# Scores beside the value product, loads reordered, another opening and a one-pass last eviction: windowed attention followed by a SoLU layer

## The chip, the cores and the metric

The kernel runs on one core of a Trainium2 chip. The metric is the device time of one execution in microseconds; several runs give a median. The engines of the core are TensorE (PE, with its weight loads shown as PEld), VectorE (DVE), ScalarE (ACT), GpSimd (POOL) and SyncE (SP, which issues the DMAs). Each works through its own list of instructions in order, and they wait for each other by semaphores.

## The reference

Eight heads of eight sequences of 576 positions attend within a window of 32 (heads 0 to 3), or to every fourth position of a window of 128 (heads 4 to 7). The result, 4608 tokens of 512 values, goes through a layer whose hidden activation is h times softmax(h), followed by a layer norm.

```python
scores = scale * np.matmul(q, k.transpose(0, 1, 3, 2))
...
scores = np.where(masks[None, :, :, :], scores, -1000000000.0)
scores = scores - np.max(scores, axis=-1, keepdims=True)
attn = np.exp(scores)
attn = attn / (np.sum(attn, axis=-1, keepdims=True) + 1e-09)
return np.matmul(attn, v).astype(np.float32)
...
h = x @ w_in                                  # 4608 x 512 x 1024
h_max = np.max(h, axis=-1, keepdims=True)
e = np.exp(h - h_max)
sm = e / (np.sum(e, axis=-1, keepdims=True) + 1e-09)
solu = h * sm
mu = np.mean(solu, axis=-1, keepdims=True)
var = np.mean((solu - mu) ** 2, axis=-1, keepdims=True)
ln = (solu - mu) / np.sqrt(var + 1e-06) * g_ln
return (ln @ w_out).astype(np.float32)        # 4608 x 1024 x 512
```

The weights come as float64.

## The kernel before

**Tiling.** The attention is cut into 32 units: a unit n is two heads of one sequence, and n % 4 of 2 and 3 are the dilated heads. The tokens are cut into 36 tiles i of 128 for the layer. Unit n's result fills a stretch of a ring (`x_hi`, `x_lo`) of two sequences; tile i reads 128 tokens of it over all four units of a sequence. Matrix products of the layer are done in three terms (high by high, high by low, low by high part), so a tile has 24 matmuls of 512 columns for `w_in` and 24 for `w_out`.

**Words.** The program is written out as a list of words, and each word issues the instructions of one small function (the table `one`, line 494). For a unit n: `q` and `v` load it on SP; `S` (line 175) are its scores, 80 small matmuls of 64 rows by 32 columns, into PSUM banks 2 and 3; `mask`, `max`, `sum`, `inv`, `norm`, `turn` are VectorE's; `sub` is POOL's from unit 4 on; `exp` ScalarE's; `V` (line 253), 96 small matmuls (80 for a dilated unit) into banks 4 to 7, multiplies the turned weights by the values; `xh` (ScalarE) and `xl` (VectorE) put the result into the ring. For a tile i: `ha` to `hd` are the matmuls with `w_in` into banks 0 and 1, six each; `peak` (VectorE) finds the row's maximum, `e` (ScalarE) the exponentials, `gate` (VectorE) h times e with its sum, `mid` takes the mean off (VectorE, for tiles 0 to 3 ScalarE), giving `t`; `var` (ScalarE and POOL) the variance; `t` (TensorE) transposes the tile into banks 3 and 4; `th` (ScalarE) and `tl` (VectorE) take its high and low parts; `o` is the product with `w_out` into bank 2, `out` scales it (ScalarE) and stores it (SP).

**Order.** Nothing is reordered: the order of the words is the order on each engine. `INIT` is the order of the first loads. `OPENING` interleaves the conversion of the weights with the attention of the first ten units and with tiles 0 to 5. From tile 6 on the loop at line 520 runs `STEP` for each tile, where n is the unit whose scores are due in this step, m the one whose scores were due in the step before, i the tile and j = i - 1. A step in which no unit is due leaves its words out. Units 10 to 31 have their scores in steps 6 to 11, 13 to 20 and 22 to 29 (line 515). Tile 35 runs `LAST`, and `END` closes.

**Weights.** A block b of 128 x 512 float64 weights (0 to 7 of `w_in`, 8 to 15 of `w_out`) is turned into a float32 high and low part from its bits: `low` and `abs` on ScalarE, `sign`, `clamp` and `join` on VectorE, `hi` on ScalarE (for blocks of `w_out` after `gain`), and the low part by `LOW_DIFF`: for a letter m by two products with plus and minus the identity on TensorE (`diff`, with `neg` preparing the minus) and a copy on ScalarE (`lo`), for a letter p by a subtraction on POOL (`lo`, line 484).

**The end.** Tile 35's product goes to bank 5, and `moe_out_last` (line 401) scales its left half on ScalarE and its right half on VectorE and stores each.

Of the kernel before, what the change touches and what calls it, by code (L numbers as in the profile page):

```python
# [14 lines left out]
AF = mybir.ActivationFunctionType  # L15
ALU = mybir.AluOpType
AX = mybir.AxisListType

B, H, S, D = 8, 8, 576, 64
# [23 lines left out]
REBIAS = 2.0**16  # L43
F64_MIN = REBIAS * float(np.array(0x38000000, np.uint32).view(np.float32))
F64_MAX = REBIAS * float(np.array(0x47EFFFFF, np.uint32).view(np.float32))
LOW_DIFF = 'mmmmmmmmpppppppp'
FIRST = 6
INIT = "q0 ib m w0 w1 v0 i g q1 w2 w3 v1 q2 w4 w5 v2 q3 v3"
OPENING = (
# [26 lines left out]
)  # L76
STEP = "ha.i hb.i S.n q.n mask.n max.n sub.n hc.i hd.i V.m v.m peak.i exp.n sum.n inv.n e.i gate.i mid.i xh.m xl.m var.i norm.n turn.n o.j t.i th.i tl.i out.j"
LAST = "ha.i hb.i hc.i hd.i peak.i e.i gate.i mid.i oa.j t.i oz.j th.i tl.i out.j var.i"
END = "o.j outz.j"

# [2 lines left out]
def windowed_attention_then_solu_kernel(  # L83
# [13 lines left out]
    nc = tc.nc  # L97
# [16 lines left out]
    mask_sb = const.tile([P, 2, NS * WQ], BF16, name="mask_sb")  # L114
# [11 lines left out]
    ps_last = banks[:, 5, :]  # L126
# [25 lines left out]
    def w_part(b):  # L152

        if b < 8:
            return w_i[:, b // 2, b % 2]
        return w_o[:, b - 8]
# [134 lines left out]
    ms = {}  # L291
# [109 lines left out]
    def moe_out_last(i):  # L401

        m = DO // 2
        rows = slice(i * P, i * P + P)
        ob = moe.tile([P, DO], F32, name="ob", bufs=1)
        left, right = ob[:, :m], ob[:, m:]
        nc.scalar.activation(out=left, in_=ps_last[:, :m], func=AF.Copy, scale=ms[i]["rstd"])
        nc.vector.tensor_scalar(
            out=right, in0=ps_last[:, m:], scalar1=ms[i]["rstd"], scalar2=None, op0=ALU.mult
        )  # L410
        nc.scalar.dma_start(out=out[rows, :m], in_=left)
        nc.sync.dma_start(out=out[rows, m:], in_=right)
        del ms[i]

    cv = {}
# [1 line left out]
    def hi(b):  # L417
        return w_part(b)[:, 0, :]
# [48 lines left out]
    def conv_hi(b):  # L467
        if b < 8 or LOW_DIFF[b] == "p":
            nc.scalar.copy(out=hi(b), in_=cv[b]["mag"])
        else:  # L470
            nc.scalar.activation(out=hi(b), in_=cv[b]["mag"], func=AF.Copy, scale=gain(b))
# [6 lines left out]
    def conv_lo(b):  # L478
        lo = w_part(b)[:, 1, :]
        kind = LOW_DIFF[b]  # L480
        if kind == "m":
# [14 lines left out]
        "i": lambda _: nc.sync.dma_start(out=id_sb, in_=ident),  # L496
        "ib": lambda _: nc.sync.dma_start(out=id_bf, in_=ident_bf),
        "g": lambda _: nc.sync.dma_start(out=g_sb, in_=g_ln),
        "m": lambda _: nc.sync.dma_start(out=mask_sb, in_=mask),
        "neg": lambda _: nc.scalar.mul(out=minus, in_=id_sb, mul=-1.0),  # L500
        "abs": conv_abs, "low": conv_low, "clamp": conv_clamp, "sign": conv_sign,
        "join": conv_join, "gain": conv_gain, "hi": conv_hi, "diff": conv_diff, "lo": conv_lo,
# [5 lines left out]
        "peak": moe_peak, "e": moe_exp, "gate": moe_gate, "mid": moe_centre, "var": moe_var,  # L508
        "t": moe_t, "th": moe_th, "tl": moe_tl, "o": moe_o, "out": moe_out,
        "oa": lambda i: moe_o(i, 0, 21), "oz": lambda i: moe_o(i, 21), "outz": moe_out_last,  # L510
    }
    fronts = {}
# [3 lines left out]

    for word in (INIT + " " + "".join(OPENING)).split():
        name = word.rstrip("0123456789")
        one[name](int(word[len(name) :] or 0))
    for i in range(FIRST, NTILE + 1):  # L520
        front, back = fronts.get(i), fronts.get(i - 1)
        of = {"n": front, "m": back, "i": i if i < NTILE else None, "j": i - 1}
        order = END if i == NTILE else LAST if i == NTILE - 1 else STEP
        for word in order.split():
# [71 lines left out]
```

## Time and profile before

| | |
|---|---|
| median of 3 runs | 567.88 us (567.01 to 571.52) |
| the profiled execution | 567.52 us |
| its span on the core | 565.7 us |
| mean granted TensorE clock | 0.982 |
| busy: TensorE, VectorE, ScalarE, POOL | 531.3, 358.2, 237.3, 110.6 us |
| DMA | 51.66 MB, 91 GB/s over the span |

A row of the timeline gives the start and the duration in us, the engine, the line of the kernel, the operation, what it writes and reads, and how many were merged; in brackets stands how long the engine was idle before it and what ended that. A row of the chain of waits gives start, duration and what it was. A row of the groups gives the number of instructions, their busy time, the mean in ns of one, and idle time before them. "issue" is time in which an engine waited for nothing that the profile shows. In the page's slices each figure stands for a fortieth of the span (14.1 us), for engines the busy tenths.

### The profile page before, as it was taken

The page shows a single profiled execution, that of the slowest core. Times are in us where ns is not written, and L with a number is a line of the kernel's source. Part 1 is how long each engine was busy: PE and PEld are TensorE (multiplying, and loading weights), DVE is VectorE, ACT ScalarE, POOL GpSimd, SP SyncE. Part 2 cuts the span into 40 slices and gives each one's busy share as a digit, 9 for nine tenths or more (in the row PEclk, how much of TensorE's full clock was granted, in tenths as well). Part 3 has the DMA queues.
Part 4 walks back from the last instruction along what each step waited for, and adds up shares of the span by engine and source line. Part 5 has one row for each costly group of instructions (what it writes and reads, how often), then busy time and mean ns, then how long its engine had stood idle before and what let it go on. Part 6 is the DMA issues. An engine that isn't in the chain of part 4 may idle for free.

```text
span 565.7 us, 16593 instructions
## 1 busy us (share of the span) xinstructions
PE 531.3 (94%) x7424; PEld 422.9 (75%) x7424; DVE 358.2 (63%) x555; ACT 237.3 (42%) x386; POOL 110.6 (20%) x256
## 2 busy tenths in 40 slices
PE   2775799899999999999999999999999999999997
PEld 1443588678888888888888888888888888888885
DVE  2989865576667766567667766567667766533342
ACT  3679754334344333433344333433344333433232
POOL 0002451123112222112112222112112222111111
PEclk9799889899999999999999999999999999999999
DMA  8976102332322233112222222123321000001001
GB/s 304 399 287 237 57 1 93 110 103 93 93 93 92 93 93 93 48 64 93 92 93 93 93 92 93 48 65 93 93 93 48 21 21 21 20 19 38 19 20 37
DMA packets 22103, 51.66 MB, mean 91 GB/s; under 512 B 2704, under 2 KB 3216, under 8 KB 22032
## 3 DMA queue, kind: packets, MB, share of 16 engines
q1 hardware_dynamic: 21888, 50.48, 26.4%
q8 instruction: 58, 0.95, 0.7%
q10 hardware_dynamic: 144, 0.13, 0.1%
q14 instruction: 13, 0.11, 0.1%
HBM read 41.16 MB, written 9.44 MB: 89 GB/s over the span
## 4 chain that ended last, share of the span: by engine, by line
PE 88%; DVE 5%; ACT 3%; issue 2%; DMA 1%; SPq 1%; ACTq 0%
PE banks L299 36%; PE banks L387 36%; PE banks L357 5%; PE banks L265 5%; PE banks L191 5%; DMA id_sb<-ident 1%; DVE x_lo L286 1%; DVE low L450 1%; DVE mag L458 1%; ACT x_hi L283 1%; PE banks L475 1%; DVE mag L443 1%; ACT low L437 0%; ACT w_i L482 0%; DVE nmax L310 0%
## 5 line engine op out<-in xcount | busy, mean ns | idle before, releaser
L299 PE MATMUL banks<-w_i,x_hi 128*128 128x512 f32 x576 | 188.9, 409 | 8.3 <-DVE mu L324 7.7
L387 PE MATMUL banks<-w_o,th 128*128 128x512 f32 x576 | 183.0, 401 | 0.0
L299 PEld LDWEIGHTS banks<-w_i,x_hi 128*128 128x128 f32 x576 | 105.1, 192 | 31.6 <-DVE mu L324 8.1
L387 PEld LDWEIGHTS banks<-w_o,th 128*128 128x128 f32 x576 | 107.0, 189 | 23.9
L299 PE MATMUL banks<-w_i,x_lo 128*128 128x512 f32 x288 | 115.0, 399 | 0.6 <-DVE x_lo L286 0.5
L387 PE MATMUL banks<-w_o,tl 128*128 128x512 f32 x288 | 112.8, 395 | 0.0
L310 DVE TENSOR_REDUCE nmax<-banks 128x1 f32<-128x1024 f32 x36 | 44.1, 1224 | 66.9 <-PE banks L299 66.9
L230 ACT ACTIVATE sm<-sm 128x640 f32<-128x640 f32 x32 | 23.5, 737 | 132.0 <-POOL sm L226 128.6
L317 ACT ACTIVATE e<-banks,nmax 128x1024 f32<-128x1024 f32 x36 | 40.2, 1117 | 65.9 <-DVE nmax L310 62.9
L372 DVE TENSOR_TENSOR tl<-banks,th 128x512 fp32r<-128x512 f32 x72 | 46.4, 685 | 32.3 <-ACT th L364 32.3
L299 PEld LDWEIGHTS banks<-w_i,x_lo 128*128 128x128 f32 x288 | 55.1, 191 | 14.3 <-DVE x_lo L286 1.4
L226 POOL TENSOR_TENSOR sm<-sm,mx 128x640 f32<-128x640 f32 x28 | 35.4, 1263 | 151.0 <-DVE mx L217 150.9
L387 PEld LDWEIGHTS banks<-w_o,tl 128*128 128x128 f32 x288 | 54.5, 189 | 12.8
L341 ACT ACTIVATE e<-t 128x1024 f32<-128x1024 f32 x36 | 38.2, 1061 | 49.6 <-DVE t L336 49.5
L205 DVE TENSOR_TENSOR sm<-banks,mask_sb 128x640 f32<-128x640 f32 x28 | 23.1, 824 | 54.5 <-PE banks L191 54.4
L364 ACT CAST th<-banks 128x512 fp32r<-128x512 f32 x72 | 38.8, 590 | 36.8 <-PE banks L357 36.7
L324 DVE CUSTOM_DVE_ANT_0 t<-banks,e 128x1024 f32<-128x1024 f32 x36 | 44.0, 1223 | 15.1 <-ACT e L317 12.0
L265 PEld LDWEIGHTS banks<-pt,vt 32*64 32x64 f32 x2816 | 33.8, 130 | 16.8 <-issue 9.0
L265 PE MATMUL banks<-pt,vt 32*64 32x64 f32 (+3 forms) x2816 | 37.3, 227 | 4.7 <-DVE pt L249 3.6
L191 PEld LDWEIGHTS banks<-kt,qt 64*32 64x32 f32 x2560 | 29.0, 109 | 15.0 <-issue 14.2
L357 PE MATMUL banks<-id_sb,t 128*128 128x128 f32 x288 | 37.5, 273 | 0.5 <-DVE x_lo L286 0.5
L357 PEld LDWEIGHTS banks<-id_sb,t 128*128 128x128 f32 x288 | 33.6, 141 | 5.8 <-DVE x_lo L286 0.8
(54 smaller groups left out, 469.5 us busy)
## 6 DMA issues: line engine op xcount, KB each, us to landing
vt<-vw SPq DMA_DIRECT2D x32, 384.0 KB, 3.6
kt<-kT SPq DMA_DIRECT2D x32, 312.0 KB, 3.1
qt<-qT SPq DMA_DIRECT2D x32, 296.0 KB, 4.1
out<-ob SPq DMA_DIRECT2D x35, 256.0 KB, 2.0
t<-w_in SPq DMA_DIRECT2D x6, 512.0 KB, 6.8
t<-w_out SPq DMA_DIRECT2D x4, 512.0 KB, 6.8
raw<-w_out SPq DMA_DIRECT2D x4, 512.0 KB, 4.7
raw<-w_in SPq DMA_DIRECT2D x2, 512.0 KB, 8.4
```

What stands on the lines that cost most here:

```text
L191: nc.tensor.matmul(out=ps_s[WIN * c : WIN * c + WIN, h, WQ * i : WQ * i + WQ], lhsT=qt[D * h : D * h + D, q0 : q0 + WIN], rhs=kt[D * h : D ...
L226: eng.tensor_tensor(out=st[n]["sm"], in0=st[n]["sm"], in1=wide(mx), op=ALU.subtract)
L265: nc.tensor.matmul(out=ps_x[D * h : D * h + D, c, c0 : c0 + k1 - k0], lhsT=vt[WIN * c : WIN * c + WIN, i, D * h : D * h + D], rhs=pt[WIN * ...
L299: nc.tensor.matmul(out=ps_h[:, half, :], lhsT=a[:, kt, xs], rhs=w_i[:, kt, half, part, :], start=(kt == 0 and k == 0), stop=(kt == KT - 1 ...
L310: nc.vector.tensor_reduce(out=nmax, in_=h, axis=AX.X, op=ALU.max, negate=True)
L317: nc.scalar.activation(out=e, in_=h, func=AF.Exp, bias=nmax, scale=1.0, accum_out=se)
L324: nc.vector.tensor_tensor_reduce(out=t, in0=h, in1=ms[i]["e"], scale=1.0, scalar=0.0, op0=ALU.mult, op1=ALU.add, accum_out=mu,)
L341: nc.scalar.activation(out=e, in_=t, func=AF.Square, accum_out=sq)
L357: nc.tensor.transpose(out=ps[:, f, :], in_=ms[i]["t"][:, k * P : k * P + P], identity=id_sb)
L364: nc.scalar.copy(out=th[:, 4 * c : 4 * c + 4], in_=ps_t[c].rearrange("p (f q) -> p f q", q=P))
L372: nc.vector.tensor_tensor(out=tl[:, fs], in0=ps_t[c].rearrange("p (f q) -> p f q", q=P), in1=ms[i]["th"][:, fs].bitcast(F32), op=ALU.subtract,
L387: nc.tensor.matmul(out=ps_o if i < NTILE - 1 else ps_last, lhsT=a[:, f, :], rhs=w_o[:, f, part, :], start=k == 0, stop=k == 3 * FT - 1,)
```

## The change

- `STEP`: `V.m` moves from behind `hd.i` to right behind `S.n`. `xh.m` moves ahead of `exp.n`, `xl.m` ahead of `sum.n`. `sum.n` and `inv.n` move ahead of `peak.i`. `v.m` comes ahead of `q.n` on SP. `var.i` comes behind `norm.n` and `turn.n`, which changes nothing on its own engines.
- `INIT`: the first weight block `w0` is loaded first; the mask comes in two halves, the second later; `g` comes later.
- `OPENING`: another order of nearly the same words, starting with the conversion of block 0; unit 3 goes ahead of unit 2; `diff6` and `diff7` are gone.
- `LOW_DIFF`: the low parts of blocks 6 and 7 are subtracted on POOL.
- `moe_out_last`: one ScalarE pass over the whole width, and two stores of it.

```diff
--- before.py
+++ after.py
@@ -43,38 +43,38 @@
 REBIAS = 2.0**16
 F64_MIN = REBIAS * float(np.array(0x38000000, np.uint32).view(np.float32))
 F64_MAX = REBIAS * float(np.array(0x47EFFFFF, np.uint32).view(np.float32))
-LOW_DIFF = 'mmmmmmmmpppppppp'
+LOW_DIFF = 'mmmmmmpppppppppp'
 FIRST = 6
-INIT = "q0 ib m w0 w1 v0 i g q1 w2 w3 v1 q2 w4 w5 v2 q3 v3"
+INIT = "w0 q0 ib m0 i w1 v0 q1 w2 w3 v1 m1 q2 w4 w5 v2 g q3 v3"
 OPENING = (
-    "neg0 S0 q4 max0 low0 abs0 sign0 clamp0 low1 sub0 abs1 join0 w6 exp0 "
-    "sign1 hi0 sum0 clamp1 inv0 S1 q5 join1 w7 norm0 hi1 diff0 max1 low2 "
-    "abs2 turn0 lo0 sign2 low3 V0 v4 clamp2 abs3 sign3 xh0 join2 w8 clamp3 "
-    "hi2 sub1 join3 w9 exp1 S2 q6 xl0 hi3 sum1 diff1 low4 max2 abs4 "
-    "diff2 inv1 lo1 sign4 low5 norm1 diff3 lo2 clamp4 abs5 turn1 lo3 join4 w10 "
-    "V1 v5 sub2 hi4 sign5 exp2 clamp5 xh1 sum2 low6 xl1 abs6 inv2 hc0 "
-    "low7 sign6 abs7 norm2 diff4 clamp6 turn2 lo4 join6 low8 V2 v6 sign7 hi6 "
-    "clamp7 S3 q7 abs8 join5 w11 xh2 join7 sign8 ha0 hi7 max3 hi5 xl2 "
-    "sub3 diff6 clamp8 exp3 join8 w12 diff7 lo6 sum3 gain8 diff5 inv3 lo7 norm3 "
-    "low10 lo5 turn3 low11 sign10 V3 v7 low9 sign11 abs10 sign9 xh3 clamp10 abs11 "
-    "xl3 abs9 clamp11 hd0 join10 w14 hi8 clamp9 gain10 lo8 hb0 hi10 join11 w15 "
-    "low12 lo10 peak0 gain11 abs12 S5 q9 join9 w13 e0 sign12 clamp12 gain9 gate0 "
-    "hi11 hi9 join12 hc1 lo11 low14 mask5 mid0 ha1 sign14 low15 lo9 max5 S4 "
-    "q8 var0 sign15 hd1 low13 sub5 mask4 abs14 hb1 abs15 sign13 abs13 t0 peak1 "
-    "gain12 th0 clamp14 clamp15 e1 clamp13 join14 join15 gain14 gate1 gain15 hi12 join13 hc2 "
-    "hi14 lo12 tl0 mid1 hd2 lo14 max4 gain13 ha2 hi15 sub4 hi13 var1 hb2 "
-    "lo15 exp4 t1 peak2 lo13 exp5 th1 sum4 o0 sum5 e2 inv4 tl1 norm4 "
-    "gate2 turn4 hc3 out0 inv5 mid2 norm5 S7 q11 var2 turn5 V4 v8 mask7 "
-    "ha3 xh4 max7 xl4 hd3 sub7 t2 exp7 o1 th2 sum7 inv7 tl2 norm7 "
-    "V5 v9 out1 S6 q10 turn7 xh5 xl5 hb3 mask6 max6 o2 peak3 sub6 "
-    "e3 exp6 gate3 sum6 V7 v11 out2 inv6 mid3 norm6 hc4 turn6 xh7 S8 "
-    "q12 var3 xl7 V6 v10 mask8 max8 ha4 xh6 sub8 xl6 t3 hd4 th3 "
-    "exp8 hb4 tl3 sum8 o3 peak4 inv8 e4 norm8 turn8 gate4 out3 mid4 hc5 "
-    "var4 t4 ha5 th4 hd5 tl4 hb5 S9 q13 peak5 V8 v12 mask9 e5 "
-    "max9 o4 xh8 gate5 sub9 xl8 exp9 mid5 sum9 var5 inv9 norm9 t5 out4 "
-    "turn9 th5 tl5 "
+    "low0 abs0 sign0 clamp0 join0 w6 S0 q4 hi0 neg0 max0 low1 sub0 abs1 "
+    "sign1 exp0 clamp1 sum0 S1 q5 join1 w7 low2 diff0 inv0 max1 hi1 low3 "
+    "norm0 diff1 abs3 sign3 abs2 clamp3 turn0 lo0 lo1 join3 w9 sub1 hi3 low4 "
+    "sign2 diff3 exp1 clamp2 sign4 low5 sum1 abs5 join2 w8 lo3 abs4 inv1 V0 "
+    "v4 sign5 hi2 norm1 S3 q7 xh0 clamp5 turn1 low7 xl0 abs7 join5 w11 "
+    "V1 v5 max3 hi5 xh1 clamp4 sub3 xl1 exp3 S2 q6 join4 w10 diff2 "
+    "sum3 hi4 max2 lo2 inv3 low6 ha0 sub2 abs6 norm3 exp2 sign6 turn3 diff5 "
+    "sum2 clamp6 lo5 inv2 low9 V3 v7 join6 abs9 norm2 hc0 hi6 sign7 xh3 "
+    "lo6 turn2 xl3 low10 clamp7 V2 v6 sign9 abs10 join7 xh2 sign10 hi7 xl2 "
+    "lo7 diff4 clamp9 low11 clamp10 lo4 join9 w13 abs11 hb0 sign11 low8 clamp11 join10 "
+    "w14 abs8 gain9 sign8 gain10 clamp8 hd0 join11 w15 hi9 join8 w12 gain11 S4 "
+    "q8 lo9 peak0 gain8 hi10 mask4 e0 lo10 max4 S5 q9 hi11 gate0 sub4 "
+    "hi8 low13 mask5 ha1 lo11 low14 mid0 hc1 sign13 low15 lo8 t0 var0 hd1 "
+    "sign14 low12 sign15 hb1 abs13 sign12 abs14 clamp13 abs15 peak1 abs12 th0 clamp14 clamp15 "
+    "clamp12 e1 join13 join14 gain13 gate1 gain14 hi13 join15 ha2 hi14 lo13 mid1 join12 "
+    "gain15 lo14 tl0 hc2 gain12 hi15 max5 hb2 hi12 lo15 exp4 hd2 var1 sum4 "
+    "lo12 inv4 t1 peak2 sub5 o0 th1 norm4 e2 tl1 exp5 turn4 sum5 gate2 "
+    "V4 v8 out0 inv5 ha3 xh4 norm5 mid2 xl4 S6 q10 turn5 var2 hc3 "
+    "mask6 V5 v9 max6 hd3 xh5 sub6 xl5 S7 q11 exp6 hb3 mask7 sum6 "
+    "t2 max7 o1 th2 inv6 sub7 peak3 norm6 e3 tl2 exp7 turn6 sum7 V6 "
+    "v10 out1 gate3 o2 xh6 inv7 norm7 mid3 xl6 var3 turn7 V7 v11 out2 "
+    "ha4 xh7 xl7 S8 q12 hc4 mask8 max8 t3 sub8 hb4 th3 hd4 tl3 "
+    "exp8 sum8 o3 peak4 inv8 e4 norm8 turn8 gate4 out3 mid4 hc5 var4 t4 "
+    "ha5 th4 tl4 hb5 S9 q13 hd5 mask9 max9 V8 v12 peak5 sub9 o4 "
+    "xh8 e5 xl8 exp9 gate5 sum9 mid5 inv9 var5 t5 norm9 th5 turn9 out4 "
+    "tl5 "
 )
-STEP = "ha.i hb.i S.n q.n mask.n max.n sub.n hc.i hd.i V.m v.m peak.i exp.n sum.n inv.n e.i gate.i mid.i xh.m xl.m var.i norm.n turn.n o.j t.i th.i tl.i out.j"
+STEP = "ha.i hb.i S.n V.m mask.n max.n sub.n xh.m exp.n xl.m v.m q.n hc.i hd.i sum.n inv.n peak.i e.i gate.i mid.i norm.n turn.n var.i o.j t.i th.i tl.i out.j"
 LAST = "ha.i hb.i hc.i hd.i peak.i e.i gate.i mid.i oa.j t.i oz.j th.i tl.i out.j var.i"
 END = "o.j outz.j"
 
@@ -403,13 +403,9 @@
         m = DO // 2
         rows = slice(i * P, i * P + P)
         ob = moe.tile([P, DO], F32, name="ob", bufs=1)
-        left, right = ob[:, :m], ob[:, m:]
-        nc.scalar.activation(out=left, in_=ps_last[:, :m], func=AF.Copy, scale=ms[i]["rstd"])
-        nc.vector.tensor_scalar(
-            out=right, in0=ps_last[:, m:], scalar1=ms[i]["rstd"], scalar2=None, op0=ALU.mult
-        )
-        nc.scalar.dma_start(out=out[rows, :m], in_=left)
-        nc.sync.dma_start(out=out[rows, m:], in_=right)
+        nc.scalar.activation(out=ob, in_=ps_last, func=AF.Copy, scale=ms[i]["rstd"])
+        nc.scalar.dma_start(out=out[rows, :m], in_=ob[:, :m])
+        nc.sync.dma_start(out=out[rows, m:], in_=ob[:, m:])
         del ms[i]
 
     cv = {}
@@ -496,7 +492,7 @@
         "i": lambda _: nc.sync.dma_start(out=id_sb, in_=ident),
         "ib": lambda _: nc.sync.dma_start(out=id_bf, in_=ident_bf),
         "g": lambda _: nc.sync.dma_start(out=g_sb, in_=g_ln),
-        "m": lambda _: nc.sync.dma_start(out=mask_sb, in_=mask),
+        "m": lambda d: nc.sync.dma_start(out=mask_sb[:, d], in_=mask[:, d]),
         "neg": lambda _: nc.scalar.mul(out=minus, in_=id_sb, mul=-1.0),
         "abs": conv_abs, "low": conv_low, "clamp": conv_clamp, "sign": conv_sign,
         "join": conv_join, "gain": conv_gain, "hi": conv_hi, "diff": conv_diff, "lo": conv_lo,
```

## The prediction

> **What bounds the kernel now.** I read the page first, then the chain of waits through the steady steps, then the timeline of one steady step engine by engine, and last the opening. The page says that TensorE is the bound:
>
> ```profile
> PE 531.3 (94%) x7424; PEld 422.9 (75%) x7424; DVE 358.2 (63%) x555; ACT 237.3 (42%) x386; POOL 110.6 (20%) x256
> ...
> PE   2775799899999999999999999999999999999997
> ...
> GB/s 304 399 287 237 57 1 93 110 103 93 93 93 92 93 93 93 48 64 93 92 93 93 93 92 93 48 65 93 93 93 48 21 21 21 20 19 38 19 20 37
> ```
>
> TensorE is busy 531.3 of 565.7 us, and the 34 us that it is not lie almost all in the first eight of 40 slices. In the chain of waits the steady part is one unbroken row of matmuls:
>
> ```profile
> 199.72 2.78 PE banks L299 x12
> ...
> 214.22 2.78 PE banks L299 x12
> ...
> 228.59 5.49 PE banks L299 x24
> ...
> 241.73 2.77 PE banks L299 x12
> ...
> 254.89 2.78 PE banks L299 x12
> ...
> 508.38 5.51 PE banks L299 x24
> ...
> 520.35 5.50 PE banks L299 x24
> ```
>
> Each line is the start of a step (its first products with `w_in`). A step with scores S and value product V lasts 14.50 us with an undilated V (199.72 to 214.22) and 14.37 with a dilated one (214.22 to 228.59); with V alone 13.14, with S alone 13.16, with neither 11.97. No other engine appears between them. So a step costs what TensorE issues in it, as long as everything else is ready in time. How near "in time" is shows in one step, first VectorE:
>
> ```profile
> 189.09 0.82 DVE L205 TENSOR_TENSOR sm<-banks,mask_sb 128x640 f32<-128x640 f32 x1 [2.33 <-PE banks L191]
> ...
> 191.99 1.23 DVE L310 TENSOR_REDUCE nmax<-banks 128x1 f32<-128x1024 f32 x1 [1.15 <-PE banks L299]
> 193.13 0.81 DVE L234 TENSOR_REDUCE rs<-sm 128x10 f32<-128x640 f32 x1
> ...
> 194.18 0.22 DVE L239 RECIPROCAL rs<-rs 128x10 f32<-128x10 f32 x1
> ...
> 196.00 0.75 DVE L336 TENSOR_SCALAR t<-t,mu 128x1024 f32<-128x1024 f32 x1
> ```
>
> and the other engines in the same step:
>
> ```profile
> 187.94 1.04 PE L191 MATMUL banks<-kt,qt 64*32 64x64 f32 x80
> ...
> 190.92 1.26 POOL L226 TENSOR_TENSOR sm<-sm,mx 128x640 f32<-128x640 f32 x1 [5.65 <-DVE mx L217]
> ...
> 192.21 0.74 ACT L230 ACTIVATE sm<-sm 128x640 f32<-128x640 f32 x1 [5.70 <-POOL sm L226]
> ...
> 198.46 1.03 PEld L357 LDWEIGHTS banks<-id_sb,t 128*128 128x128 f32 x8
> ...
> 202.44 1.04 PE L191 MATMUL banks<-kt,qt 64*32 64x64 f32 x80
> ```
>
> `peak` (L310) goes ahead of `sum` (L234). The centred `t` is done at 196.75 (196.00 + 0.75), and its transposes begin at 198.46: a slack of 1.71 us.
>
> **The change, the steady step.** Two things are moved. On TensorE, V stands right behind S. On VectorE, `sum` and `inv` now stand ahead of `peak`, and `xl` ahead of both.
>
> *VectorE, the term that decides.* VectorE takes its work in order. `sum` needs `exp`, which ends at 192.95 (192.21 + 0.74), 5.01 us after S began; that chain (mask, max, Pool's subtract, exp) is unchanged. The sum to the end of the reciprocal took 1.27 us (193.13 to 194.40). So `peak` can start no earlier than 192.95 + 0.03 + 1.27 + 0.03 = 194.28, against 191.99 now: 2.29 later. Queued behind it on VectorE are gate, mid, norm, turn and tl; ScalarE's `e` and `var` and TensorE's `t` wait for them. From the start of `peak` to the finished `t` it is 4.76 us (191.99 to 196.75), all of it dependent work. So `t` is finished at 199.04, and its transposes can begin at about 199.10. The slack of 1.71 is gone.
>
> What hides nothing here should be said too. `xh` and `xl` of the last unit now go ahead of `exp` and `sum`:
>
> ```profile
> L286 DVE TENSOR_TENSOR x_lo<-banks,x_hi 128x576 fp32r<-128x576 f32 x32 | 31.5, 986 | 4.3 <-ACT x_hi L283 4.3
> L283 ACT CAST x_hi<-banks 128x576 fp32r<-128x576 f32 x32 | 29.2, 911 | 3.1 <-PE banks L265 2.9
> ```
>
> V ends about 2.2 us after S began, so `xh` ends at 3.2 and `xl` at 4.2, under Pool's 4.24 and exp's 5.01. They cost nothing, and Pool's subtract covers them; if V were 1 us late, `xl` would push `sum`. The loads on SP (v before q) now wait for V's end, some 1.2 us later than q's wait for S; their data is needed four units later, so nothing waits.
>
> *TensorE.* The neighbours S and V exist in the opening of the trace already, and V stands alone in the step above:
>
> ```profile
> 133.13 1.04 PE L191 MATMUL banks<-kt,qt 64*32 64x64 f32 x80
> 134.10 1.20 PE L265 MATMUL banks<-pt,vt 32*64 32x32 f32 x96
> 135.34 0.70 PE L387 MATMUL banks<-w_o,th 128*128 128x512 f32 x2
> ```
> ```profile
> 191.88 1.10 PEld L265 LDWEIGHTS banks<-pt,vt 32*64 32x64 f32 x96 [0.35 <-issue]
> ...
> 193.00 0.30 PEld L387 LDWEIGHTS banks<-w_o,th 128*128 128x128 f32 x2
> ```
>
> S holds TensorE for 0.97 us (133.13 to 134.10) but makes a step 1.19 longer (13.16 - 11.97): 0.22 goes on leaving the large tiles and coming back. One such passage is saved. Behind S, V takes 1.24 us, alone 1.12: 0.12 is lost. Net gain 0.1 us a step; 0 to 0.2 are its bounds. TensorE alone would reach the transposes at 198.36.
>
> *Both together.* The transposes wait until 199.10, and from there to the next S it is 3.98 us as now (198.46 to 202.44). The step becomes 199.10 - 187.94 + 3.98 = 15.14 us whatever V it holds. By the line that deals units to steps, units 10 to 31 have their scores in steps 6 to 11, 13 to 20 and 22 to 29, and their values one step later: 20 steps with both (11 undilated, 9 dilated) and steps 13 and 22 with S alone. Sum: 11 x (15.14 - 14.50) + 9 x (15.14 - 14.37) + 2 x (15.14 - 13.16) = 7.0 + 6.9 + 4.0 = **+17.9 us**. An error of 0.15 in the chain, the size of its hand-overs, is 3.3 us over 22 steps.
>
> *Instruction pages.* TensorE's program comes by DMA:
>
> ```profile
> q8 instruction: 58, 0.95, 0.7%
> ```
> ```profile
> 38.44 0.38 PE L191 MATMUL banks<-kt,qt 64*32 64x64 f32 x18 [1.32 <-issue]
> ```
> ```profile
> 100.94 0.33 PE L191 MATMUL banks<-kt,qt 64*32 64x64 f32 x11 [1.97 <-issue]
> ...
> 102.00 1.01 PE L299 MATMUL banks<-w_i,x_hi 128*128 128x512 f32 x2
> ```
>
> 58 pages for 14,848 loads and matmuls: 256 each. Both rows are an S right behind a V, stopped in its midst for 1.32 and 1.97 us by nothing that the profile shows, as one would see if a page were used up before the next had come. After the longer stop two matmuls of this size took 1.01 us, against 0.70 in the row at 135.34: a lowered clock. A pair of S and V has 320 to 352 instructions, more than a page. It holds two page ends if the first lies in its first 64 (dilated) or 96 instructions: (96 x 11 + 64 x 9) / 256 = 6.4 of the 20 pairs. The pair at 133.13 did not stop, and a page that is asked for early enough comes in time, so I count 4 of them, at 1.65 us (the mean of the two rows). The stop falls late in the pair, in V: TensorE then reaches the transposes at 200.0, 0.9 behind the chain's 199.10. So **+4 us**; bounds 0 and +11 (six full stops, with the lowered clock).
>
> [...]
>
> **The opening.**
>
> ```profile
> 10.40 0.31 ACT L500 ACTIVATE minus<-id_sb 128x128 fp32r<-128x128 f32 x1 [8.40 <-DMA id_sb<-ident]
> ```
> ```profile
> t<-w_in SPq DMA_DIRECT2D x6, 512.0 KB, 6.8
> ```
> ```profile
> 50.14 1.55 DVE L443 TENSOR_SCALAR mag<-mag 128x512 f32<-128x512 f32 x1
> ```
> ```profile
> L443 DVE TENSOR_SCALAR mag<-mag 128x512 f32<-128x512 f32 x16 | 7.7, 493 | 0.0
> ```
> ```profile
> 78.02 0.71 PE L387 MATMUL banks<-w_o,th 128*128 128x512 f32 x2
> ```
> ```profile
> 142.03 2.78 PE banks L299 x12
> ```
>
> ScalarE stands 8.40 us before `neg0` and takes its first weight block at 10.7. In the new order w0 is the first load and `low0` the first work. Issued at 0.7 with the median 6.8 us to landing it is there at 7.5, 3 us sooner; with nothing ahead of it perhaps at 4.5, 6 sooner. The other loads come no faster than before (the page's second slice moves 399 GB/s), so part of it is waited away again; I keep 2. `lo6` and `lo7` go from TensorE and ScalarE to Pool: a clamp took 1.55 us in place of a mean 0.49 while Pool subtracted, so one such hit, +1. From `o0` (78.02) to the first steady step (142.03) the old order loses 1.97 us to the stop above and after it 0.15 us a matmul while the clock is low (an estimate: eleven matmuls, 1.6 us); the new one has no S next to a V there: -3.6. Sum -2 + 1 - 3.6 = **-4.6 us**; bounds -10 (the whole early start and no hit) and +3 (no early start, three hits).
>
> **The last eviction.**
>
> ```profile
> 562.17 0.47 ACT L407 ACTIVATE ob<-banks,rstd 128x256 f32<-128x256 f32 x1 [3.86 <-PE banks L387]
> ...
> 563.19 0.33 SPq L412 DMA_DIRECT2D out<-ob  x1
> ```
> ```profile
> L397 ACT ACTIVATE ob<-banks,rstd 128x512 f32<-128x512 f32 x35 | 24.5, 701 | 16.7 <-PE banks L387 13.3 <-issue 3.4
> ```
>
> The halves run one after the other; the second store is issued at 563.19. One pass of 0.70 lets both go at about 562.9: -0.3 us.
>
> **Sum.** The profiled execution took 567.5 us (span 565.7 and 1.8 around it); the median of the runs is 0.4 above. 567.5 + 17.9 + 4 - 4.6 - 0.3 = 584.5; I say **584 us**. Its own range is 574 to 595 (chain +-3.3, pages 0 to +11, opening -10 to +3, not all at one end).
>
> **The rivals.**
>
> *The cover holds* (the other side). If `peak` starts less than 1.7 us later than now, the transposes don't wait, and the steady part only gains its 0.1 x 20 = 2 us: 567.5 - 2 - 4.6 - 0.3 = 560.6; with one page stop paid in full, 562. For it: the slack of 1.71 is real, and 2.29 is only 0.58 beyond. Against it: `exp` can't end sooner, since it depends on S alone, and the rows add up without a gap. Chance 0.12.
>
> *The opening pays it back.* The first quarter holds 34 us of idle TensorE. If the new order recovers 18 of it instead of 4.6, the time is 584 - 13 = 571. Against: VectorE is nearly full there and has the same work. Chance 0.10.
>
> *A page stop in nearly every pair.* 20 x 0.9 = 18 in place of 4, or the lowered clock in the eight worst: 598. For it: the two that stopped are 2 of the 4 such pairs in the opening. Against: the count of page ends. Chance 0.10.
>
> **How the numbers follow.** The forecast has 0.68. The range 568 to 597 holds it and the second rival; it leaves out the first and most of the third. About 1% (5.7 us) is what a measurement of this kernel can tell from no change. Faster than 562.2: 0.09, most of the first rival. Within 1%: 0.11, the rest of it and most of the second. Slower: 0.80.
>
> **What would show it.** Right: steady steps of 15.1 us; an idle time of TensorE at L357 put down to `t` L336, some 0.7 us in each of 20 steps and 2 in two; `peak` starting right behind the reciprocal; three to six waits on "issue" within V. Wrong: L357 without idle time and steps of 14.4, or the first steady step later than 145 or earlier than 130.

## The result, and the profile after

The changed kernel takes 591.05 us (median of 4 runs, 587.35 to 593.28); the kernel before, on the same chip, takes 568.62. The ratio is 1.0386, with a 95% interval of 1.035 to 1.0422: it is slower. The profiled execution took 591.32 us with a span of 589.5, against 567.52 and 565.7.

The page of the kernel after:

```profile
PE 538.9 (91%) x7418; PEld 428.6 (73%) x7418; DVE 359.2 (61%) x554; ACT 236.2 (40%) x384; POOL 108.8 (18%) x258
...
PE   3586699999998999999999999998999899999997
...
PE 67%; DVE 16%; ACT 6%; issue 4%; DMA 3%; POOL 3%; DVEq 0%; ACTq 0%
```

TensorE's own work has grown by only 7.6 us. The last line, the shares of the chain that ended last, tells more. VectorE holds 16% of the chain, ScalarE 6%, POOL 3% and "issue" 4%. The steady steps have become a chain through four engines, broken here and there by stops of TensorE. The chain of waits shows both:

```profile
141.00 2.77 PE banks L299 x12
...
155.97 2.79 PE banks L299 x12
...
161.66 1.27 POOL sm L226
...
165.00 1.09 DVE nmax L310
170.77 2.79 PE banks L299 x12
...
185.57 2.78 PE banks L299 x12
...
190.28 1.50 issue
...
192.19 4.54 PE banks L299 x12
...
202.31 0.87 PE banks L357 x8
203.18 2.73 PE banks L299 x12
...
246.92 2.78 PE banks L299 x12
...
261.73 2.75 PE banks L299 x12
...
276.50 2.77 PE banks L299 x12
```

As in the prediction, a line of twelve products of L299 begins a step; the one at 192.19 is the step's second twelve. The steps of 155.97 and 170.77, both with a dilated V, last 14.80 us each, and the one of 261.73, with an undilated V, 14.77: the length no longer depends on TensorE's work. The step at 185.57 lasts 17.61, with a stop of 1.50 in it and twelve products that take 4.54. The step at 246.92 has scores alone and lasts 14.81, where 13.16 had been enough.

The first line divides the difference. Up to tile 6 it took 141.00 us (142.03 before), from there to the end 448.5 (589.5 - 141.00) against 423.7 (565.7 - 142.03). So the opening is 1.0 shorter and the rest 24.8 longer, which makes the 23.8 of the spans.

VectorE, in the timeline of the step that starts at 155.97:

```profile
163.72 0.82 DVE L234 TENSOR_REDUCE rs<-sm 128x10 f32<-128x640 f32 x1 [0.53 <-ACT sm L230]
...
164.78 0.22 DVE L239 RECIPROCAL rs<-rs 128x10 f32<-128x10 f32 x1
164.92 1.16 DVE L310 TENSOR_REDUCE nmax<-banks 128x1 f32<-128x1024 f32 x1
...
168.87 0.75 DVE L336 TENSOR_SCALAR t<-t,mu 128x1024 f32<-128x1024 f32 x1
```

and TensorE in it:

```profile
158.69 1.04 PE L191 MATMUL banks<-kt,qt 64*32 64x64 f32 x80
...
169.68 1.09 PE L357 MATMUL banks<-id_sb,t 128*128 128x128 f32 x8 [0.41 <-DVE t L336]
...
173.49 0.73 PE L191 MATMUL banks<-kt,qt 64*32 64x64 f32 x52
```

`peak` (L310) starts with the end of the reciprocal, 6.23 us after S began, and the transposes wait 0.41 us for `t` (with an undilated V 0.27). The list of waits of the kernel after gives the totals (us, times, longest):

```profile
PE banks L265 <- issue: 8.4, 6, 1.9
PE banks L357 <- DVE t L336: 6.8, 13, 1.4
...
PE banks L299 <- issue: 2.7, 4, 1.3
```

Of the ten stops at L265 and L299 one (0.74 us) lies in the opening and nine in the steady part. The 13 waits for `t` are one in each step with scores that has no stop: 11 with both products and the two with scores alone.

### The profile page after: what moved, and what is told of

It reads as the page before. It is cut to its first block, busy times and chain, and to the rows that moved or that the text cites. A ratio compares the mean times of both kernels' runs of the same rounds, so it can differ in the third digit from the quotient of the medians.

```text
span 589.5 us, 16557 instructions
## 1 busy us (share of the span) xinstructions
PE 538.9 (91%) x7418; PEld 428.6 (73%) x7418; DVE 359.2 (61%) x554; ACT 236.2 (40%) x384; POOL 108.8 (18%) x258
## 4 chain that ended last, share of the span: by engine, by line
PE 67%; DVE 16%; ACT 6%; issue 4%; DMA 3%; POOL 3%; DVEq 0%; ACTq 0%
PE banks L299 30%; PE banks L387 22%; PE banks L357 6%; PE banks L191 5%; PE banks L265 4%; DVE t L324 3%; POOL sm L226 3%; DVE nmax L310 3%; ACT e L317 3%; DVE mx L217 2%; DVE sm L205 2%; DVE rs L234 2%; ACT sm L230 2%; DVE t L336 2%; DMA raw<-w_in 1%
## 5 line engine op out<-in xcount | busy, mean ns | idle before, releaser
L299 PE MATMUL banks<-w_i,x_hi 128*128 128x512 f32 x576 | 195.2, 421 | 6.7 <-DVE mu L324 5.7
L387 PE MATMUL banks<-w_o,th 128*128 128x512 f32 x576 | 180.1, 396 | 0.0
L299 PEld LDWEIGHTS banks<-w_i,x_hi 128*128 128x128 f32 x576 | 108.4, 198 | 31.4 <-DVE mu L324 6.2
L387 PEld LDWEIGHTS banks<-w_o,th 128*128 128x128 f32 x576 | 108.3, 189 | 25.0
L299 PE MATMUL banks<-w_i,x_lo 128*128 128x512 f32 x288 | 117.6, 408 | 2.0 <-issue 2.0
L299 PEld LDWEIGHTS banks<-w_i,x_lo 128*128 128x128 f32 x288 | 56.8, 197 | 16.3 <-issue 2.8
L283 ACT CAST x_hi<-banks 128x576 fp32r<-128x576 f32 x32 | 29.4, 918 | 95.6 <-PE banks L265 95.6
L310 DVE TENSOR_REDUCE nmax<-banks 128x1 f32<-128x1024 f32 x36 | 43.0, 1195 | 33.0 <-PE banks L299 33.0
L286 DVE TENSOR_TENSOR x_lo<-banks,x_hi 128x576 fp32r<-128x576 f32 x32 | 31.4, 981 | 34.8 <-ACT x_hi L283 34.7
L265 PE MATMUL banks<-pt,vt 32*64 32x64 f32 (+3 forms) x2816 | 39.3, 232 | 13.4 <-issue 8.4
L265 PEld LDWEIGHTS banks<-pt,vt 32*64 32x64 f32 x2816 | 35.1, 135 | 20.9 <-issue 12.3
L357 PE MATMUL banks<-id_sb,t 128*128 128x128 f32 x288 | 38.1, 275 | 6.8 <-DVE t L336 6.8
L357 PEld LDWEIGHTS banks<-id_sb,t 128*128 128x128 f32 x288 | 32.6, 141 | 15.8 <-DVE t L336 12.9
```

The costliest lines, as they stand in the source:

```text
L265: nc.tensor.matmul(out=ps_x[D * h : D * h + D, c, c0 : c0 + k1 - k0], lhsT=vt[WIN * c : WIN * c + WIN, i, D * h : D * h + D], rhs=pt[WIN * ...
L299: nc.tensor.matmul(out=ps_h[:, half, :], lhsT=a[:, kt, xs], rhs=w_i[:, kt, half, part, :], start=(kt == 0 and k == 0), stop=(kt == KT - 1 ...
L310: nc.vector.tensor_reduce(out=nmax, in_=h, axis=AX.X, op=ALU.max, negate=True)
L357: nc.tensor.transpose(out=ps[:, f, :], in_=ms[i]["t"][:, k * P : k * P + P], identity=id_sb)
L387: nc.tensor.matmul(out=ps_o if i < NTILE - 1 else ps_last, lhsT=a[:, f, :], rhs=w_o[:, f, part, :], start=k == 0, stop=k == 3 * FT - 1,)
```

## The experiments

Three questions: do the late `peak` and the stops stand beside each other as two costs, does the place of the page ends make the stops, and what is the opening worth? Times are medians beside the kernel before on the same chip. "Steady part" is the time from tile 6's first products to the end of the span, as worked out above: 423.7 before, 448.5 after.

**`peak` first again.** The changed kernel with only this undone:

```diff
-... hc.i hd.i sum.n inv.n peak.i e.i gate.i ...
+... hc.i hd.i peak.i sum.n inv.n e.i gate.i ...
```

> The changed kernel, with peak back ahead of sum and inv on VectorE; V stays right behind S. My theory (two separate costs: the late peak, 10.6 us in the steady part of the changed profile, and page stops with the lowered clock, 13.9 us): no idle time of TensorE at L357 put down to t, steps without a stop of 14.4 us, still about nine stops on issue in S-V pairs; about 579 us. Rival (the stops are a consequence of the late peak, for instance because TensorE's sequencer runs less far ahead when it waits): the stops go too, about 566 us. Rival (the late peak costs nothing and all the loss is in the stops): no change, 591 us.

575.23 us (572.57 to 579.24), ratio 1.0134 (1.008 to 1.0187). TensorE has no idle time before L357 any more, and the chain is again matmuls alone:

```profile
154.23 2.79 PE banks L299 x12
...
161.96 5.58 PE banks L387 x24
167.54 0.87 PE banks L357 x8
168.41 2.78 PE banks L299 x12
```

This step with a dilated V lasts 14.18 (14.37 before), those with an undilated one 14.31 (14.50). So S and V side by side save 0.19 us a step. The stops are still there, and nearly as many:

```profile
PE banks L265 <- issue: 6.9, 7, 1.5
```

Seven steps are longer than 14.31 or 14.17 by more than 0.7 us; all excesses sum to 14.7. The steady part is 435.0 (574.8 - 139.81), 13.5 less than after. The late `peak` is one cost, and the stops are another that doesn't hang on it.

**V apart again.** The late `peak` stays, V goes back behind the products with `w_in`, and with it `xh` and `xl` behind `mid`:

```diff
-ha.i hb.i S.n V.m mask.n max.n sub.n xh.m exp.n xl.m v.m q.n hc.i hd.i sum.n inv.n peak.i ... mid.i norm.n
+ha.i hb.i S.n mask.n max.n sub.n exp.n hc.i hd.i V.m v.m q.n sum.n inv.n peak.i ... mid.i xh.m xl.m norm.n
```

> The changed kernel, with V and xh, xl back behind hd as before, and sum and inv still ahead of peak. My theory: no stop on issue in the steady steps, TensorE waits at L357 for t as in the changed kernel, 0.3 to 0.4 us in 20 steps and 1.4 in two; steps of 14.8 us; about 577 us. Rival (the late peak hurts only together with V in front): steps of 14.4, about 567 us. Rival (stops come with the late peak): 591 us.

585.77 us (584.8 to 587.08), ratio 1.0321 (1.0287 to 1.0355). The stops of the steady part are gone, as expected, but the time is 9 us above what was expected. The steps last 15.00 and 15.47, and the timeline shows why the second kind is longer:

```profile
170.17 1.21 DVE L286 TENSOR_TENSOR x_lo<-banks,x_hi 128x576 fp32r<-128x576 f32 x1
...
170.31 0.66 PE L357 MATMUL banks<-id_sb,t 128*128 128x128 f32 x4 [0.20 <-DVE t L336]
...
171.43 0.66 PE L357 MATMUL banks<-id_sb,t 128*128 128x128 f32 x4 [0.46 <-DVE x_lo L286]
```

The second half of the transposes goes into bank 4, which V has filled and `xl` (L286) reads. Now `xl` stands behind `t` on VectorE, so these four wait for it after waiting for `t`; by the list of waits their weight loads wait for `xl` 20 times, 9.2 us in all: in every step with both products. V in front of the step doesn't only save TensorE time; it also lets `xl` be done in time. The run therefore doesn't give the price of the late `peak` by itself.

**The old step.** Opening, loads and last eviction of the changed kernel with STEP as before.

```diff
-STEP = "ha.i hb.i S.n V.m mask.n max.n sub.n xh.m exp.n xl.m ..."
+STEP = "ha.i hb.i S.n q.n mask.n max.n sub.n hc.i hd.i V.m v.m peak.i ..."
```

> The changed kernel with the whole old STEP; opening, first loads, low parts of blocks 6 and 7 on Pool and the one-pass last eviction stay new. My theory: the steady part is that of the kernel before (423.9 us from tile 6 on), the opening 1.0 us shorter as in the changed profile, the last eviction worth nothing: 567 us, 1 to 2 below the kernel before. Rival (prediction's own figure for the opening, 4.6 us, held down by something of the new step): 563 us.

566.37 us (564.45 to 568.5), ratio 0.9973 (0.9951 to 0.9996): about 1.5 us (0.2 to 2.8), less than a third of the 4.9 predicted. The steady part is as before, 423.8 (566.7 - 142.93). The new opening's timeline shows where its early start goes:

```profile
28.97 0.37 PE L191 MATMUL banks<-kt,qt 64*32 64x64 f32 x2 [3.93 <-issue]
...
29.38 0.82 DVE L217 TENSOR_REDUCE mx<-banks 128x10 f32<-128x640 f32 x1 [3.41 <-PE banks L191]
...
29.99 0.78 ACT L433 ACTIVATE low<-t,below 128x512 int32<-128x512 uint16 x1 [5.83 <-DMA t<-w_in]
```

The last two matmuls of S3 stop for 3.93 us, VectorE stands 3.41 us for their result, and at the same place ScalarE stands 5.83 us for block 7 of `w_in`.

**The mask of unit 3 on VectorE.** In the kernel of the run before, unit 3's mask is added on VectorE. TensorE then has four instructions fewer ahead of these last matmuls, so that S3 should end before the page does:

```diff
-PE_MASK = (0, 1, 2, 3)
+PE_MASK = (0, 1, 2)
-... max3 ...
+... mask3 max3 ...
```

> The kernel with the old step and the new opening, in which the mask of unit 3 is added on VectorE (and its subtraction done on Pool) and not on TensorE. That takes four instructions from TensorE ahead of the last scores of unit 3, which stopped for 3.93 us on a page there, with its two last matmuls left. The page theory: the scores of unit 3 end ahead of the page end, max of unit 3 starts 2 to 3 us sooner, and the opening's own gain comes out: 563 to 565 us. Rival (the loads of the weight blocks set the opening's pace at that place: ScalarE waits 5.83 us for one): no change, 566 us.

568.79 us (565.74 to 572.5), ratio 1.0006 (0.9984 to 1.0028): a miss. The timeline:

```profile
26.82 0.82 DVE L217 TENSOR_REDUCE mx<-sm 128x10 f32<-128x640 f32 x1
...
29.19 1.69 PE L265 MATMUL banks<-pt,vt 32*64 32x32 f32 x96 [3.88 <-issue]
...
30.26 0.76 ACT L433 ACTIVATE low<-t,below 128x512 int32<-128x512 uint16 x1 [5.60 <-DMA t<-w_in]
...
35.23 1.06 PE L191 MATMUL banks<-kt,qt 64*32 64x64 f32 x50 [3.11 <-issue]
```

`max3` did come 2.6 us sooner. But the stop only moved on to V1 (3.88 us), the next one, in S2, is 3.11 us instead of 0.67, and ScalarE waits for its block as before. What holds the opening is in the loads (ScalarE's 5.60 us) and in the stops on "issue" (3.88 and 3.11); how much each holds stays open.

**Page ends out of the pairs.** The kernel with `peak` first, in which a few scores of some units are computed twice with the same values, so that the page ends fall elsewhere. Its time holds that work.

```diff
+REPEAT = {8: 22, 9: 22, 10: 11, 11: 19, 12: 19, 13: 11, ...}
-        for i in range(NS):
-            for h in range(2):
-                for c in range(NG):
+        places = [(i, h, c) for i in range(NS) for h in range(2) for c in range(NG)]
+        for i, h, c in places[: REPEAT.get(n, 0)] + places:
```

> The kernel with peak first (V right behind S) in which some scores are computed twice, with the same values, only to move the places where TensorE's pages of 256 instructions end: 22 extra score products in each of units 8 and 9, then 11 or 19 in the units of the steady pairs, so that the first page end stands some 190 to 226 instructions into each pair and the second behind it. The page theory: no stop on issue in any of the 20 pairs, though each pair is longer; steps of 14.6 us (14.31 and 14.17 measured without a stop, and 22 or 38 extra small matmuls at 12 ns); about 570 us. Rival (a pair stops because so many small instructions come at once, wherever the pages end): at least as many stops as with peak first, 583 us or more.

571.71 us (one run), and no stop in any pair, as expected. **Page ends in every pair** is the same kernel with 128 fewer instructions of this kind ahead of tile 6 (`{9: 12, ...}` in place of `{8: 22, 9: 22, ...}`) and the same steps.

> The same as the kernel with page ends clear, but with 12 extra score products in unit 9 and none in unit 8 in place of 22 and 22, so that the first page end stands 62 to 98 instructions into each of the 20 pairs and the second also inside it. All steady pairs have the same instructions as there. The page theory: a stop of 1.2 to 2 us in each of the 20 pairs, in about half of them followed by the lowered clock; 45 us more than with page ends clear, about 615 us. Rival (stops come from the number of small instructions, or from what else loads data): the same time as with page ends clear.

610.69 us (one run), 39 us more with the same steady work. All 20 pairs stop, as expected (the 21st stop of the list below lies in the opening); the lowered clock follows in five of them (granted 0.62 from 199.00 to 203.40 behind one stop, and 1.00 from 216.90 to 219.70 behind another), where half were expected, and so it is 39 and not 45. The waits of the first kernel (us, times, longest; all of them in the opening):

```profile
PE banks L191 <- issue: 4.0, 2, 3.0
...
PE banks L265 <- issue: 0.8, 1, 0.8
```

and of the second:

```profile
PE banks L265 <- issue: 28.2, 21, 1.9
```

One pair, with a dilated V, in the timeline of the first:

```profile
160.96 1.46 PE L191 MATMUL banks<-kt,qt 64*32 64x64 f32 x118
162.35 1.08 PE L265 MATMUL banks<-pt,vt 32*64 32x64 f32 x80
```

and the same pair in the second:

```profile
162.16 1.46 PE L191 MATMUL banks<-kt,qt 64*32 64x64 f32 x118
163.55 0.71 PE L265 MATMUL banks<-pt,vt 32*64 32x64 f32 x41
165.93 0.66 PE L265 MATMUL banks<-pt,vt 32*64 32x64 f32 x39 [1.67 <-issue]
```

Count the instructions up to the stop: 118 and 41 matmuls, each with its weight load, are 318, with the semaphore instructions among them about 320. Counted in this way from the start of each trace, the matmuls in the ten traces of this case have 66 stops on "issue" longer than 0.25 us, and all 66 lie at the same place of a block of 256, within one instruction. With a page end at that place, the first page end of this pair lies 64 instructions in, and TensorE stops where the second page ends. In the first kernel the first page end lies 192 in, and the pair holds no second. That the place of the page ends makes the stops is shown.

**Both apart.** The changed kernel's STEP with the same repeated scores as in the kernel with the page ends out of the pairs (the diff is that one's). It completes the square of early or late `peak`, and page ends as they fall or out of the pairs.

> The changed kernel's STEP, with `peak` behind the sums, in which a few scores of some units are computed twice with the same values (as in the run with `peak` first and the page ends clear; its time holds that work), so that no pair of S and V has a page end among its first instructions and a second one inside. Theory, that the step with late `peak` and the page stops are two separate costs: no idle time of TensorE on 'issue' after the opening, every step with both products about 14.95 with an undilated and 15.05 with a dilated V (14.80 plus the 0.13 to 0.23 by which the added scores delay the mask), and a time 11 x 0.41 + 9 x 0.45 + 2 x 1.65 = 11.9 above the 571.7 of the run with `peak` first, 583.6 us. Rival, that a stop fills the wait for `t` and the two don't add: the time comes out at 586 or more, with waits for `t` longer than 0.5 us in the pairs that had a stop. Second rival, that stops come from the two products side by side wherever the page ends lie: about 591 to 593.

583.46 us (582.18 to 585.71), ratio 1.0264 (1.0225 to 1.0303). The chain of waits has no "issue" after the opening:

```profile
187.30 2.78 PE banks L299 x12
...
202.33 2.78 PE banks L299 x12
```

The steps last 15.03 (202.33 - 187.30) with an undilated V and 15.20 to 15.23 with most of the dilated, and the waits for `t` are in all 22 steps with scores:

```profile
PE banks L357 <- DVE t L336: 9.5, 22, 1.4
```

The total came out as expected, but by two errors: I had counted the added scores at half their length (11 entries of the list are 22 matmuls), and this run's opening was 1.8 us shorter than that of its neighbour (141.93 against 143.76). The steady parts are free of the second:

| steady part, us | page ends as they fall | out of the pairs |
|---|---|---|
| `peak` first | 435.0 | 426.1 |
| `peak` late | 448.5 | 440.4 |

Late `peak` costs 13.5 and 14.3. Clearing the page ends saves 8.9 and 8.1, and the added scores cost about 5.8 and 6.0 of their own (13 steps by some 0.23 and 7 by some 0.42), so the stops are worth 14.7 and 14.1. The two costs exist without each other, and their totals add within about 1 us. No more can be said: each figure comes from one execution, and the clock fell after four stops with late `peak` and after three with early `peak` (mean granted clock 0.959 and 0.969). Within a stopped step they overlap a little, since the transposes don't wait for `t` there.

**The kernel before, shifted.** The prediction's rows of before had two such stops in the opening. Here twenty entries of unit 5's scores are computed twice, so that the page end of the later of these pairs falls elsewhere; nothing else of the kernel before is changed.

```diff
+REPEAT = {5: 20}
```

> The kernel before with 20 scores of unit 5 computed twice, with the same values, where TensorE waits anyway: this moves the page end out of the pair V5, S6 in the opening, which stopped 1.97 us and was followed by a lowered clock. The page theory: that stop and the lowered clock after it are gone, 3 us less, about 565 us. Rival (the time lost there is won back, because something else is late by then): no change.

565.06 us (563.39 to 566.23), ratio 0.9938 (0.9914 to 0.9963). The stop of 1.97 us at 100.94 is gone, the other remains:

```profile
PE banks L191 <- issue: 1.7, 1, 1.7
```

It beats the kernel before by 0.6%, with more work on the engine that bounds it.

## Why the prediction was right, and where not

The forecast was 584 and the range 568 to 597; 591.05 lies in it, on the side that was named, and for the two causes that were named. But the sizes of the two were wrong in opposite directions, so that 584 came as near as it did is in part luck. Terms of the sum, all in us:

| | predicted | measured |
|---|---|---|
| late `peak`, side by side saving included | +17.9 | +10.6 |
| instruction pages | +4 | +13.9 |
| opening | -4.6 | -1.0 |
| last eviction | -0.3 | +0.1 |
| sum | +17.0 | +23.6 (spans: +23.8) |

- **The late `peak`.** The mechanism stood at each step: `sum` could start 5.03 us after S began (predicted 5.04), the transposes waited for `t`, and the step had one length whatever V it held. The price was mis-sized in two places of the 15.14. The chain from S to the transposes took 10.99 (169.68 - 158.69) and not 11.16, since `peak` began before the reciprocal's listed end and the hand-overs behind it were shorter. And from the transposes to the next S it was 3.81 (173.49 - 169.68), not 3.98: I had taken the 3.98 from the start of a weight load that ran beside the end of the product before it, and behind a wait in the kernel after, load and product begin together (both at 169.68; in the kernel before the load at 198.46, the product at 198.69). Together 0.34 a step: 14.80. Sum with it: 11 x 0.31 + 9 x 0.43 + 2 x 1.65 = 10.6. The idle time at L357 was 0.27 to 0.41 in a step without a stop and 1.4 in the two steps with scores alone, not 0.7 and 2.
- **Side by side.** The saving is 0.19 a step, at the upper end of the bounds 0 to 0.2, or 3.8 in all. Against that baseline (14.31 and 14.18) the late `peak` costs 14.4. The square has 14.3 where no pair stops and 13.5 where nine do. But the saving comes with the stops: with V apart the steady part had none, as before.
- **`xh` and `xl` "cost nothing".** Right as far as it went; that their earlier place was needed, as the run with V apart showed, I had not seen.
- **Instruction pages.** The step that failed is the count of the stops and what each of them costs. I took 4 of 6.4 pairs at 0.9 us beyond the chain. Nine pairs stopped, six of them for 1.23 us or more. Five have their second page end inside, which is near the count. But a pair stops also when that end comes a few instructions after it: four times the first page end lay 102 or 110 instructions in, and a stop of 0.37 to 1.26 us came among the next products. The price failed more. That a stop takes the place of the wait for `t` was right: in the step at 185.57 `t` was done at 201.53, and the transposes began at 202.15, right behind TensorE's own products. But the wait that is saved was 0.27 to 0.41 and not 0.74 (199.10 - 198.36), so most of a stop is paid. And after four stops the lowered clock (granted 0.56 from 192.20 to 195.60 and 0.60 from 297.70 to 302.00 behind two of them), which I had only in my upper bound, added 1.6 each (twelve products in 4.54 against 2.95). The nine excesses over 14.80 sum to 13.9, beyond my bound of 11. With the page ends out of the pairs, 20 pairs passed a single page end without a stop; with the page ends in every pair, two that come close together in instructions as short as these stopped all 20: 39 us for the place of the page ends alone (610.69 against 571.71).
- **The opening.** The early start came: the first conversion runs on VectorE at 7.39 us, not at 11.38. Almost all of it was waited away again, as I had said of a part; the new order meets a stop of 2.8 to 4.0 us (at 28.62 in the kernel after) in place of those that it loses. That the stop at 100.94 and the clock after it (granted 0.62 from 101.27 to 104.50) are worth some 3 us, the kernel before, shifted, bears out (2.1 to 4.9 by its interval). I had written that it has no S next to a V from `o0` on, and had not looked for pairs ahead of that, where the stops are longest. Four runs with this same opening reach tile 6 at 139.81, 141.00, 141.70 and 142.93, so the -1.0 is a size with a spread of 3 us; the run with the old step gives -1.5 for opening and eviction together.
- **The last eviction.** One pass let the second store go 0.3 us sooner (0.71 us after the pass began, against 1.02), but the first one 0.2 later (0.72 against 0.51), and side by side they took longer, as the rows of DMA issues of the kernel after show (KB, median us to landing), 2.1 and 1.9 against 1.8 and 1.7 before:

```profile
out<-ob ACTq DMA_DIRECT2D x1, 128.0 KB, 2.1
out<-ob SPq DMA_DIRECT2D x1, 128.0 KB, 1.9
```

- **The rivals.** "The cover holds" is out: the transposes wait for `t` in all 13 steps with scores that have no stop. "The opening pays it back" is out. "A page stop in nearly every pair" was wrong in its count (9 of 20) and nearer than the forecast in its price.

## What to carry to other kernels

Where a chain through several engines has a slack of 1.7 us, moving one word 2.3 us later on one of them costs in every step, and the sum of durations along the chain predicts it to a few tenths (15.14 us a step against 14.80); take the hand-overs from rows in which the waiting engine really waited. A run of some 320 short TensorE instructions holds more than one page of the program (256 by the 58 packets for 14,848 instructions): count where the 256s fall, because here two page ends within 2.9 to 3.6 us stopped the engine, and a few instructions more or less ahead of the run can be worth more than the reordering (39 us here, for 128 of them). What a reordering saves in busy time should be weighed against what it puts next to each other: here two products side by side gained 3.8 us and brought 13.9 of stops, and a word moved with them cost 14.4.

## What the runs showed of the hardware

- **In the nine pairs that stopped, 2.9 to 3.6 us passed from one page end to the first instruction behind the next.** In the step at 185.57 the timeline of the kernel after shows:

```profile
188.28 1.04 PE L191 MATMUL banks<-kt,qt 64*32 64x64 f32 x80
189.25 1.03 PE L265 MATMUL banks<-pt,vt 32*64 32x32 f32 x75
191.78 0.41 PE L265 MATMUL banks<-pt,vt 32*64 32x48 f32 x21 [1.50 <-issue]
```

The first page end lies 56 instructions into the pair, at about 188.6 (56 of S's 160 instructions); the second is at 312, and 80 and 75 matmuls with their loads are 310. TensorE goes on at 191.78. So about 3.2 us passed from the first page end until TensorE went on behind the second; for the stop at 402.86 it is 3.6 by the same working, and the other seven of the steady part lie between 2.9 and 3.5. The 256 instructions between the two last some 1.7 us of the 3.2 (188.6 to 190.28), and the stop is the other 1.50. In the opening, while the weights are loaded, stops were up to 4.0 us (at L191, with `peak` first).

- **The clock fell after some short stops and not after others.** The granted clock (the third figure from the end) in the products after the stop of 1.50 and after the one of 1.92:

```profile
192.20:195.60 3.40, 3.40 (x9) 2.70 (x10) 1.88 (x4) 1.27 (x2) 0.32 (x1) 0.56 0.74 218
405.20:408.10 2.90, 2.90 (x13) 2.38 (x14) 1.87 (x4) 1.28 (x2) 0.00 (x0) 1.00 0.66 188
```

The longer stop left the clock at 1.00 and the shorter one brought it to 0.56. What tells the two cases apart, no run here shows.
